# Agent attention with two feed-forward layers on one core: output transfers later in SyncE's order, one layer end in two pieces, a written order for the last nine half groups

## The chip, the cores and the metric

The kernel runs on one core of one Trainium2 chip. The metric is the device time of one execution in microseconds (us). Five engines work side by side, each in its own order: TensorE (PE; its weight loads are listed as PEld), VectorE (DVE), ScalarE (ACT), GpSimd (POOL) and SyncE (SP). SyncE computes nothing; here it issues transfers and passes on signals.

## The reference

For 12480 tokens of 128 values each, and 49 agent rows, all float32:

```python
a2k = softmax(scale * agents @ k.T)          # 49 x 12480
agent_v = a2k @ v                            # 49 x 128
x = softmax(scale * q @ agents.T) @ agent_v  # 12480 x 128
h = x @ w_in                                 # first layer, 128 -> 2048
x = (h / (1 + exp(-h))) @ w_out              # 2048 -> 128
h = x @ w2_in                                # second layer, 128 -> 2048
out = (h * cos(h)) @ w2_out                  # 2048 -> 128
```

The weights are float64 in memory and are split into a high and a low float32 part; so are the activations. A product of a split pair is three matmuls: high by high, low by high, high by low.

## The kernel before

The first 110 us or so load and transpose k, q and v, split the weights and do the attention. All that follows, and all that the change touches, is the two layers.

The tokens stand in 25 tiles t (22 of 512, then 416, 416 and 384). The 2048 inner values stand in 16 chunks of 128; a half group (g, k), with g = 4t + m, is two of these chunks of one tile. So a tile has eight half groups, and there are 200 in all. For each half group the first layer does `L1_h` (PE), `L1_act` (ACT, silu), `L1_hi` (ACT, high part), `L1_lo` (DVE, low part) and `L1_y` (PE, adds into the bank y1 of the tile). The second layer does, with x2 as its input, `L2_h` (PE), `L2_n` (ACT, line 789: whole turns of the cosine's argument), `L2_r` (DVE, 799: what is left of it), `L2_cos` (ACT, 808), `L2_g` (DVE, 816: times h), `L2_hi` (825, high part: DVE, but ACT for k = 1 of the last groups), `L2_lo` (POOL, 834) and `L2_y` (PE, into the bank y2).

The main loop (line 883) runs over steps s. A step does the first layer of half group s and the second layer of half group u = s - 11; a round is eight steps, one tile. Once a round the first layer of a tile ends: ACT copies the high part of bank y1 (`x2h`, 751), DVE subtracts it (`x2l`, 759). The bank y1 may be written again only when both have read it. And once a round a tile of the second layer ends (`L2_end`): DVE transposes bank y2 into tile `o` (856), and SyncE issues four transfers of `o` to the output (858). Also once a round SyncE issues two transfers that load `x3` (614).

In the main loop every product runs on half of TensorE's rows (`half`, line 621): the upper 64 rows do one stream of products, the lower 64 the same stream nine products later, side by side. [...]

```python
n = nc.sync.nop()
tc.add_manual_dep(n.ins, other[1], AFTER, reason="one row tile at a time in a bank")
tc.add_manual_dep(i.ins, n.ins.name, AFTER, reason="one row tile at a time in a bank")
```

It waits for the last product of the one half in that bank, and the first product of the other half waits for it. I call it a fence. There are about five in a step, and SyncE takes fences and transfers strictly in the order written. The kernel up to the end of the main loop stands in that written order on every engine (`tc.manual_schedule()`, opened at 220 and closed by `whole.close()` at 909).

After the main loop come nine half groups of the second layer alone (u = 191 to 199, the loop at 915), on whole rows (`whole_rows`, 734). There a scheduler sets the order on each engine.

Of the kernel before, what the change touches and what calls it, by code (L numbers as in the profile page):

```python
# [8 lines left out]
F32 = mybir.dt.float32  # L9
# [5 lines left out]
ALU = mybir.AluOpType  # L15
# [14 lines left out]
WIDE = 512  # L30
# [39 lines left out]
def agent_attention_moe_moe_kernel(ctx, tc, q, k, v, agents, w_in, w_out, w2_in, w2_out, out):  # L70
    nc = tc.nc
# [44 lines left out]
    def b32(ap):  # L116
        return ap.bitcast(F32)
# [23 lines left out]
    whole = ctx.enter_context(ExitStack())  # L141

    edge = ctx.enter_context(tc.tile_pool(name="edge", bufs=1, side="right"))
    edge.tile([128, EDGE // 4], F32, name="border")
    x3_p = ctx.enter_context(tc.tile_pool(name="x3", bufs=2, side="right"))
    late = ctx.enter_context(ExitStack())

    def after(name, bufs):
# [408 lines left out]
    with ExitStack() as ml:  # L557
# [11 lines left out]
        NL = len(widths)  # L569
        NG = NL * 4  # L570

        def toks(t):
            return widths[t]
# [10 lines left out]
        h1s, g1s, y1s, x2s, h2s, c2s, g2s, y2s = {}, {}, {}, {}, {}, {}, {}, {}  # L584
        v, sc, gp = nc.vector, nc.scalar, nc.gpsimd
# [5 lines left out]
        def wide(pool, tag, dt, g):  # L591
            return pool.tile([128, 2, WIDE], dt, tag=tag, name=tag)[:, :, :toks(g // 4)]

        last_pair, taken = [], [0]
# [26 lines left out]
        def half(x, bank, n, out, w, g, start, stop):  # L621

            assert before[0] is None or before[0][0] == x or before[0][1] != bank
            before[0] = x, bank
            rows = slice(HALF * x, HALF * x + n)
            i = nc.tensor.matmul(  # L626
                out=out, lhsT=w[rows], rhs=g[rows], start=start, stop=stop, tile_position=(HALF * x, 0)
            )
            other = writer.get((bank, 1 - x))
            if other is not None and other[0] > fenced[0]:  # L630
# [3 lines that stand above are left out]
                fenced[0] = other[0]  # L634
            writer[bank, x] = count[0], i.ins.name
            count[0] += 1
# [8 lines left out]
        def level():  # L645
            while behind:
                half(1, *behind.pop(0))
# [97 lines left out]
        def L1_end_a(g):  # L745

            if not (0 <= g < NG and g % 4 == 3):
                return
            t = g // 4
            xh = x2_p.tile([128, WIDE], F32R, tag="x2h", name="x2h")[:, :toks(t)]  # L750
            sc.copy(out=xh, in_=y1s[t])
            x2s[t] = [xh]

        def L1_end_b(g):
            if not (0 <= g < NG and g % 4 == 3):
                return
            t = g // 4
            xl = x2_p.tile([128, WIDE], F32R, tag="x2l", name="x2l")[:, :toks(t)]
            v.tensor_tensor(out=xl, in0=y1s.pop(t), in1=b32(x2s[t][0]), op=ALU.subtract)  # L759
            x2s[t].append(xl)  # L760


        def L2_h(g, k, how=whole_rows, bank=pair_bank):
            if not 0 <= g < NG:
                return
            t, m = g // 4, g % 4
            h = bank()
            xh, xl = x2s[t]
            ops = []
            for j in range(2):  # L770
                c = 4 * m + 2 * k + j
                y = h[:, j, :toks(t)]
                ops += [
                    (("h2", g, k, j), y, i2h[:, c, :], xh, True, False), (("h2", g, k, j), y, i2l[:, c, :], xh, False, False),
                    (("h2", g, k, j), y, i2h[:, c, :], xl, False, True),
                ]
            how(ops)
            h2s[g, k] = h[:, :, :toks(t)]
# [5 lines left out]
        def L2_n(g, k):  # L784
            if not 0 <= g < NG:
                return
            n = wide(n_p, "n", I32, g)
            for p in parts(g):
                sc.activation(  # L789
                    out=n[:, p], in_=h2s[g, k][:, p], func=AF.Identity, scale=1.0 / (2.0 * PI), bias=quarter  # L790
                )
            c2s[g, k] = n

        def L2_r(g, k):
            if not 0 <= g < NG:
                return
            n = c2s[g, k]
            for p in parts(g):
                v.scalar_tensor_tensor(  # L799
                    out=b32(n)[:, p], in0=n[:, p], scalar=-2.0 * PI, in1=h2s[g, k][:, p], op0=ALU.mult, op1=ALU.add  # L800
                )

        def L2_cos(g, k):
            if not 0 <= g < NG:
                return
            r = b32(c2s[g, k])
            for p in parts(g):
                sc.activation(out=r[:, p], in_=r[:, p], func=AF.Sin, bias=halfpi)  # L808

        def L2_g(g, k):  # L810
            if not 0 <= g < NG:
                return
            r, h = b32(c2s.pop((g, k))), h2s.pop((g, k))
            f = wide(g2_p, "g2", F32, g)
            for p in parts(g):
                v.tensor_tensor(out=f[:, p], in0=r[:, p], in1=h[:, p], op=ALU.mult)  # L816
            g2s[g, k] = [f]

        def L2_hi(g, k):

            if not 0 <= g < NG:
                return
            gh = wide(g2h_p, "g2h", F32R, g)
            for p in parts(g):
                (sc.copy if k and g + LAG >= NG else v.tensor_copy)(out=gh[:, p], in_=g2s[g, k][0][:, p])  # L825
            g2s[g, k].append(gh)

        def L2_lo(g, k):
            if not 0 <= g < NG:
                return  # L830
            f, gh = g2s[g, k]
            gl = wide(g2l_p, "g2l", F32R, g)
            for p in parts(g):
                i = (v if (g, k) == (NG - 1, 1) else gp).tensor_tensor(  # L834
                    out=gl[:, p], in0=f[:, p], in1=b32(gh)[:, p], op=ALU.subtract
                )
            if last_lo[0] is not None:
                tc.add_manual_dep(i.ins, last_lo.pop().ins.name, AFTER, reason="one at a time on the port to SBUF")
                last_lo.append(None)
            g2s[g, k] = [gh, gl]  # L840
# [10 lines left out]
        def L2_end(g):  # L851
            if not (0 <= g < NG and g % 4 == 3):
                return
            t = g // 4
            o = o_p.tile([128, WIDE // 32, 32], F32, tag="o", name="o")[:, :toks(t) // 32]
            v.transpose(out=o.rearrange("p b j -> p (b j)"), in_=y2s.pop(t))  # L856
            for cb in range(4):
                (nc.scalar if t == 24 and cb % 2 else nc.sync).dma_start(  # L858
                    out=out[span(t), 32 * cb:32 * cb + 32].rearrange("(b i) j -> i b j", i=32),
                    in_=o[32 * cb:32 * cb + 32],  # L860
                )

        def first_products(g):
            if g == 1:
# [12 lines left out]
        o_p = pool("o", 2, "right")  # L877
        LEAD = 2 * LAG + 1

        def at(s):  # L880
            return s // 2, s % 2

        for s in range(2 * LAG, 2 * NG + 2):
            u = s - LEAD
            steady[0] = int(u >= 3)
            if s % 8 == 2:
                swapped_in(s // 8 + 1)
            L2_h(*at(u), both_halves, bank2)
            if s % 8 == 6:
                L2_end(at(u - 4)[0])  # L890
            L2_hi(*at(u - 2))
            if s > 2 * LAG:
                L1_lo(*at(s - 2))
            L2_lo(*at(u - 2))
            L1_h(*at(s))
            if s > LEAD and s % 8 == 2:
                L1_end_a(at(s - 3)[0])
            L1_hi(*at(s - 1))
            if s > LEAD and s % 8 == 2:
                L1_end_b(at(s - 3)[0])  # L900
            L2_g(*at(u - 1))
            L2_y(*at(u - 3), both_halves)
            L1_y(*at(s - 2), both_halves)
            L2_n(*at(u))
            L2_r(*at(u))
            L1_act(*at(s))
            L2_cos(*at(u))
        level()
        whole.close()
        L1_end_a(NG - 1)  # L910
        L1_end_b(NG - 1)
        taken[0] = 2
        L2_hi(*at(2 * NG - LEAD))
        L2_lo(*at(2 * NG - LEAD))
        for s in range(2 * NG + 2, 2 * NG + LEAD + 4):
            u = s - LEAD
            L2_g(*at(u - 1))
            L2_y(*at(u - 3))
            L2_h(*at(u))
            L2_hi(*at(u - 1))  # L920
            L2_n(*at(u))
            L2_r(*at(u))
            L2_lo(*at(u - 1))
            if s % 8 == 5:
                L2_end(at(u - 3)[0])
            L2_cos(*at(u))


# [28 lines left out]
```

## Time and profile before

| | |
|---|---|
| time, three runs | 1130.25, 1131.27 (median), 1132.8 us |
| profiled execution | 1131.86 us, span of its instructions 1130.1 us |
| PE busy | 1077.7 us, 95% of the span |
| DVE busy | 919.9 us, 81% |
| ACT busy | 903.6 us, 80% |
| POOL busy | 503.2 us, 45% |
| mean granted clock of TensorE | 0.995 |

The span runs from the first to the last instruction; the rest of the execution's time lies around it. Busy is the time in which an engine worked on something; matmul ends are modelled. [...]

### The profile page before, as it was taken

Reading aid. Unit: us, or ns where it says so; the run is one execution under the profiler, and the core shown is the slowest. Engines: PE = TensorE matmul, PEld = TensorE weight load, DVE = VectorE, ACT = ScalarE, POOL = GpSimd, SP = SyncE. Lnnn points to the kernel's source line nnn. Section 1 sums busy time; section 2 is a strip of 40 time slices with the busy share of each in tenths; the row PEclk is TensorE's granted clock in tenths of the full one; section 3 lists DMA queues with packets and bytes.
Section 4 is the critical chain, followed back from the end, with each engine's and each line's share of the span. In section 5 each row is a group of like instructions: output and inputs, shape, how many; then the busy total and the mean of one; then the engine's idle time right before and its main releaser. Section 6 shows DMA issues by size and latency. Waiting matters only on the chain.

```text
span 1130.1 us, 22554 instructions
## 1 busy us (share of the span) xinstructions
PE 1077.7 (95%) x9069; PEld 931.7 (82%) x9069; DVE 919.9 (81%) x1050; ACT 903.6 (80%) x968; POOL 503.2 (45%) x251
## 2 busy tenths in 40 slices
PE   9999999999999999999999999999999999999996
PEld 5897698788888888798888888888888888888985
DVE  6877787888887888888888787888788888878876
ACT  5888887887887787788788788778878878777865
POOL 0443054444444454445454444454445444445444
PEclk9999999999999999999999999999999999999999
DMA  9872000000000000000000000000000000000000
GB/s 350 306 246 94 8 8 10 18 9 10 18 9 10 17 9 18 11 9 17 10 9 18 11 13 13 10 18 8 14 14 8 18 10 8 16 10 16 2 8 15
DMA packets 67058, 40.32 MB, mean 36 GB/s; under 512 B 52774, under 2 KB 57501, under 8 KB 66953
## 3 DMA queue, kind: packets, MB, share of 16 engines
q1 hardware_dynamic: 66152, 38.78, 11.5%
q8 instruction: 71, 1.16, 0.4%
q14 instruction: 35, 0.28, 0.1%
q10 hardware_dynamic: 800, 0.10, 0.1%
HBM read 27.58 MB, written 6.39 MB: 30 GB/s over the span
## 4 chain that ended last, share of the span: by engine, by line
PE 75%; DVE 10%; ACT 6%; SPq 4%; issue 3%; DMA 1%; POOL 0%; DVEq 0%; POOLq 0%; ACTq 0%
PE h L626 39%; PE y L626 27%; ACT n L789 5%; SPq L858 4%; DVE n L799 3%; DVE g1l L718 2%; PE h L252 2%; PE h L364 2%; DVE o L856 1%; PE y L734 1%; DVE g2h L825 1%; DVE x2l L759 1%; PE h L288 1%; PE y L351 1%; PE y L422 1%
## 5 line engine op out<-in xcount | busy, mean ns | idle before, releaser
L834 POOL TENSOR_TENSOR g2l<-g,g2h 128x1024 fp32r<-128x1024 f32 (+2 forms) x200 | 468.5, 2343 | 552.1 <-DVE g1l L718 534.9
L799 DVE SCALAR_TENSOR_TENSOR n<-n,h 128x1024 f32<-128x1024 int32 (+3 forms) x202 | 238.9, 1184 | 173.5 <-ACT n L789 170.4
L626 PE MATMUL h<-x2h,i2h 64*128 64x512 f32 (+1 forms) x764 | 296.7, 388 | 35.7 <-SPq L631 34.8
L789 ACT ACTIVATE n<-h,quarter 128x1024 int32<-128x1024 f32 (+3 forms) x202 | 219.5, 1088 | 112.8 <-PE h L626 82.8
L626 PE MATMUL y<-g1h,o1h 64*128 64x512 f32 (+2 forms) x768 | 297.9, 388 | 1.4 <-DVE x2l L759 0.4
L626 PE MATMUL y<-g1h,o1l 64*128 64x512 f32 (+2 forms) x768 | 296.3, 386 | 0.0
L626 PE MATMUL y<-g2h,o2l 64*128 64x512 f32 (+1 forms) x752 | 296.0, 394 | 0.0
L626 PE MATMUL y<-g2h,o2h 64*128 64x512 f32 (+1 forms) x752 | 294.3, 391 | 0.0
L626 PE MATMUL h<-x2h,i2l 64*128 64x512 f32 (+1 forms) x764 | 293.7, 384 | 0.0
L626 PE MATMUL h<-x2l,i2h 64*128 64x512 f32 (+1 forms) x764 | 293.4, 384 | 0.0
L808 ACT ACTIVATE n<-n,halfpi 128x1024 f32<-128x1024 f32 (+3 forms) x202 | 226.9, 1124 | 79.7 <-DVE n L799 79.6
L718 DVE TENSOR_TENSOR g1l<-g,g1h 128x1024 fp32r<-128x1024 f32 (+2 forms) x200 | 238.2, 1191 | 4.3 <-ACT g1h L710 1.6
L816 DVE TENSOR_TENSOR g<-n,h 128x1024 f32<-128x1024 f32 (+3 forms) x202 | 237.4, 1176 | 4.4 <-ACT n L808 3.7
L626 PE MATMUL y<-g2l,o2h 64*128 64x512 f32 (+1 forms) x752 | 233.4, 390 | 0.0
L626 PE MATMUL y<-g1l,o1h 64*128 64x512 f32 (+2 forms) x768 | 232.9, 383 | 0.2 <-DVE g1l L718 0.2
L710 ACT CAST g1h<-g 128x1024 fp32r<-128x1024 f32 (+2 forms) x200 | 203.0, 1015 | 0.2
L703 ACT ACTIVATE g<-h 128x1024 f32<-128x1024 f32 (+2 forms) x200 | 199.6, 998 | 2.4 <-DVE g1l L718 1.2
L626 PEld LDWEIGHTS h<-x2h,i2h 64*128 64x128 f32 x764 | 141.0, 185 | 55.9 <-SPq L631 43.2
L626 PE MATMUL h<-pT,w2h 49*128 49x512 f32 (+2 forms) x400 | 158.2, 397 | 0.0
L626 PEld LDWEIGHTS y<-g1h,o1h 64*128 64x128 f32 x768 | 142.4, 185 | 16.8 <-DVE x2l L759 11.4
L626 PE MATMUL h<-x,w2h 49*128 49x512 f32 (+2 forms) x400 | 155.7, 391 | 0.0
L626 PEld LDWEIGHTS h<-x2l,i2h 64*128 64x128 f32 x764 | 140.9, 184 | 13.0
(145 smaller groups left out, 1921.4 us busy)
## 6 DMA issues: line engine op xcount, KB each, us to landing
qraw<-in_q_dram SPq DMA_DIRECT2D x12, 512.0 KB
vraw<-in_v_dram SPq DMA_DIRECT2D x12, 512.0 KB
kraw<-in_k_dram SPq DMA_DIRECT2D x11, 512.0 KB
out_dram<-o SPq DMA_DIRECT2D x88, 64.0 KB
x<-pT SPq DMA_DIRECT2D x44, 98.0 KB
wraw<-in_moe_w_in_dram SPq DMA_DIRECT2D x8, 512.0 KB
wraw<-in_moe_w_out_dram SPq DMA_DIRECT2D x8, 512.0 KB
kraw<-in_k_dram SPq DMA_DIRECT2D x2, 256.0 KB
```

Source lines behind the costliest of these rows:

```text
L252: nc.tensor.transpose(out=pt[:, g, p * s:p * s + p], in_=r[:, h * g + s, :], identity=ident[:p, :p])
L364: nc.tensor.matmul(out=ps[:p, NA * i:NA * i + 2 * NA], lhsT=xt[:, i // h, p * (i % h):p * (i % h) + p], rhs=ag2, start=True, stop=True,)
L626: i = nc.tensor.matmul(out=out, lhsT=w[rows], rhs=g[rows], start=start, stop=stop, tile_position=(HALF * x, 0))
L703: sc.activation(out=f, in_=h1s.pop((g, k))[:, :, :toks(g // 4)], func=AF.Silu)
L710: sc.copy(out=gh, in_=g1s[g, k][0])
L718: i = v.tensor_tensor(out=gl, in0=f, in1=b32(gh), op=ALU.subtract)
L789: sc.activation(out=n[:, p], in_=h2s[g, k][:, p], func=AF.Identity, scale=1.0 / (2.0 * PI), bias=quarter)
L799: v.scalar_tensor_tensor(out=b32(n)[:, p], in0=n[:, p], scalar=-2.0 * PI, in1=h2s[g, k][:, p], op0=ALU.mult, op1=ALU.add)
L808: sc.activation(out=r[:, p], in_=r[:, p], func=AF.Sin, bias=halfpi)
L816: v.tensor_tensor(out=f[:, p], in0=r[:, p], in1=h[:, p], op=ALU.mult)
L834: i = (v if (g, k) == (NG - 1, 1) else gp).tensor_tensor(out=gl[:, p], in0=f[:, p], in1=b32(gh)[:, p], op=ALU.subtract)
L858: (nc.scalar if t == 24 and cb % 2 else nc.sync).dma_start(out=out[span(t), 32 * cb:32 * cb + 32].rearrange("(b i) j -> i b j", i=32), in_ ...
```

## The change

The diff has these parts. `L2_end` keeps the transpose; the four transfers move into a new `L2_out`, which the main loop calls at the end of the same step, so that on SyncE they stand behind four more fences. The copy and the subtraction at the end of the first layer become two instructions each, one for each half of the tile's columns (`cuts`). The last nine half groups are now inside the written order (`whole.close()` stands at the very end), and that order is a new one: in each step `L2_y` of u - 3, then `L2_h` of u, then `L2_n` of u, `L2_cos` of u - 1, `L2_g`, `L2_hi` and `L2_lo` of u - 2. The pool of `x3` gets another rule for the reuse of its buffers. ACT's two output transfers of the last tile are the same.

```diff
--- before.py
+++ after.py
@@ -142,7 +142,7 @@
 
     edge = ctx.enter_context(tc.tile_pool(name="edge", bufs=1, side="right"))
     edge.tile([128, EDGE // 4], F32, name="border")
-    x3_p = ctx.enter_context(tc.tile_pool(name="x3", bufs=2, side="right"))
+    x3_p = ctx.enter_context(tc.tile_pool(name="x3", bufs=2, side="right", reuse_waits="tile"))
     late = ctx.enter_context(ExitStack())
 
     def after(name, bufs):
@@ -748,7 +748,8 @@
                 return
             t = g // 4
             xh = x2_p.tile([128, WIDE], F32R, tag="x2h", name="x2h")[:, :toks(t)]
-            sc.copy(out=xh, in_=y1s[t])
+            for c in cuts(t):
+                sc.copy(out=xh[:, c], in_=y1s[t][:, c])
             x2s[t] = [xh]
 
         def L1_end_b(g):
@@ -756,9 +757,14 @@
                 return
             t = g // 4
             xl = x2_p.tile([128, WIDE], F32R, tag="x2l", name="x2l")[:, :toks(t)]
-            v.tensor_tensor(out=xl, in0=y1s.pop(t), in1=b32(x2s[t][0]), op=ALU.subtract)
+            y = y1s.pop(t)
+            for c in cuts(t):
+                v.tensor_tensor(out=xl[:, c], in0=y[:, c], in1=b32(x2s[t][0])[:, c], op=ALU.subtract)
             x2s[t].append(xl)
 
+        def cuts(t):
+            h = toks(t) // 2
+            return slice(0, h), slice(h, toks(t))
 
         def L2_h(g, k, how=whole_rows, bank=pair_bank):
             if not 0 <= g < NG:
@@ -852,13 +858,21 @@
             if not (0 <= g < NG and g % 4 == 3):
                 return
             t = g // 4
-            o = o_p.tile([128, WIDE // 32, 32], F32, tag="o", name="o")[:, :toks(t) // 32]
-            v.transpose(out=o.rearrange("p b j -> p (b j)"), in_=y2s.pop(t))
+            outs[t] = o_p.tile([128, WIDE // 32, 32], F32, tag="o", name="o")[:, :toks(t) // 32]
+            v.transpose(out=outs[t].rearrange("p b j -> p (b j)"), in_=y2s.pop(t))
+
+        def L2_out(g):
+            if not (0 <= g < NG and g % 4 == 3):
+                return
+            t = g // 4
+            o = outs.pop(t)
             for cb in range(4):
-                (nc.scalar if t == 24 and cb % 2 else nc.sync).dma_start(
+                (nc.scalar if t == NL - 1 and cb % 2 else nc.sync).dma_start(
                     out=out[span(t), 32 * cb:32 * cb + 32].rearrange("(b i) j -> i b j", i=32),
                     in_=o[32 * cb:32 * cb + 32],
                 )
+
+        outs = {}
 
         def first_products(g):
             if g == 1:
@@ -905,25 +919,33 @@
             L2_r(*at(u))
             L1_act(*at(s))
             L2_cos(*at(u))
+            if s % 8 == 6:
+                L2_out(at(u - 4)[0])
         level()
-        whole.close()
+        taken[0] = 2
+        TAIL = 2 * NG + 2 - LEAD
+        u = TAIL - 1
         L1_end_a(NG - 1)
+        L2_g(*at(u))
         L1_end_b(NG - 1)
-        taken[0] = 2
-        L2_hi(*at(2 * NG - LEAD))
-        L2_lo(*at(2 * NG - LEAD))
-        for s in range(2 * NG + 2, 2 * NG + LEAD + 4):
-            u = s - LEAD
-            L2_g(*at(u - 1))
+        L2_hi(*at(u - 1))
+        L2_lo(*at(u - 1))
+        for u in range(TAIL, 2 * NG + 3):
             L2_y(*at(u - 3))
             L2_h(*at(u))
-            L2_hi(*at(u - 1))
             L2_n(*at(u))
+            if u > TAIL:
+                L2_cos(*at(u - 1))
+            if u > TAIL + 1:
+                L2_g(*at(u - 2))
+            if u % 8 == 2:
+                L2_end(at(u - 3)[0])
+                L2_out(at(u - 3)[0])
+            if u > TAIL:
+                L2_hi(*at(u - 2))
+                L2_lo(*at(u - 2))
             L2_r(*at(u))
-            L2_lo(*at(u - 1))
-            if s % 8 == 5:
-                L2_end(at(u - 3)[0])
-            L2_cos(*at(u))
+        whole.close()
 
 
 # ---- launch: one core; inputs and outputs as the reference has them ----
```

How this moves instructions at the end of the first layer, on DVE, in the middle of the main loop. `x2l` is the low part, `x2h` the high part that ACT copies; in brackets what an instruction waits for. Before:

```order
L718 TENSOR_TENSOR g1l_8008<-g1_7921,g1h_7951 128x1024
L759 TENSOR_TENSOR x2l_8023<-y1_7505,x2h_8019 128x512 [waits Activation_49]
L816 TENSOR_TENSOR g2_8025<-n_7983,h2_7924 128x1024 [waits Pool_49]
L799 SCALAR_TENSOR_TENSOR n_8057<-n_8057,h2_7992 128x1024 [waits Activation_49]
L825 CAST g2h_8077<-g2_8025 128x1024 [waits DVE_49]
```

And in the changed kernel (another tile, the same place in the round):

```order
L718 TENSOR_TENSOR g1l_7494<-g1_7407,g1h_7437 128x1024
L762 TENSOR_TENSOR x2l_7510<-y1_6991,x2h_7505 128x256 [waits PE_49,Activation_49]
L762 TENSOR_TENSOR x2l_7510<-y1_6991,x2h_7505 128x256
L822 TENSOR_TENSOR g2_7513<-n_7469,h2_7410 128x1024 [waits Pool_49]
L805 SCALAR_TENSOR_TENSOR n_7545<-n_7545,h2_7478 128x1024 [waits Activation_49]
```

One subtraction of 512 columns has become two of 256; the first waits for ACT, the second has no wait of its own.

On PE in the last nine half groups, from the middle of `L2_h` of u = 193. `h2_14469`, `h_14492` and `h2_14509`, `h_14532` are u = 193 and 194 in the one and the other kernel, `y2_...` is the output bank, `g2h` and `g2l` the high and low part. Before:

```order
L734 MATMUL h2_14469<-x2h_14407,i2l_75 128x384
L734 MATMUL h2_14469<-x2l_14409,i2h_74 128x384
L734 MATMUL h_14492<-x2h_14407,i2h_74 128x384
L734 MATMUL h_14492<-x2h_14407,i2l_75 128x384
L734 MATMUL h_14492<-x2l_14409,i2h_74 128x384
L734 MATMUL h_14492<-x2h_14407,i2h_74 128x384
L734 MATMUL h_14492<-x2h_14407,i2l_75 128x384
L734 MATMUL y2_14188<-g2h_14453,o2h_76 128x416
```

And now:

```order
L734 MATMUL h2_14509<-x2h_14454,i2l_75 128x384
L734 MATMUL h2_14509<-x2l_14459,i2h_74 128x384
L734 MATMUL y2_14232<-g2h_14521,o2h_76 128x416
L734 MATMUL y2_14232<-g2h_14521,o2l_77 128x416
L734 MATMUL y2_14232<-g2h_14521,o2h_76 128x416
L734 MATMUL y2_14232<-g2h_14521,o2l_77 128x416
L734 MATMUL y2_14232<-g2l_14523,o2h_76 128x416 x2
L734 MATMUL h_14532<-x2h_14454,i2h_74 128x384
```

All six products of `L2_y` of u = 191 now stand ahead of `L2_h` of u = 194; five of the six of that `L2_h` stood ahead of them before.

On ACT, a little later (`h_14492` to `h2_14545` are u = 194 to 196, `h2_14585` and `h_14608` are u = 196 and 197). Before:

```order
L789 ACTIVATE n_14501<-h_14492,quarter_67 128x2x384
L808 ACTIVATE n_14478<-n_14478,halfpi_68 128x2x384
L808 ACTIVATE n_14501<-n_14501,halfpi_68 128x2x384
L789 ACTIVATE n_14531<-h2_14522,quarter_67 128x2x384
L825 CAST g2h_14499<-g2_14484 128x2x384
L808 ACTIVATE n_14531<-n_14531,halfpi_68 128x2x384
L789 ACTIVATE n_14554<-h2_14545,quarter_67 128x2x384
```

And now:

```order
L795 ACTIVATE n_14592<-h2_14585,quarter_67 128x2x384
L814 ACTIVATE n_14569<-n_14569,halfpi_68 128x2x384
L795 ACTIVATE n_14615<-h_14608,quarter_67 128x2x384
L814 ACTIVATE n_14592<-n_14592,halfpi_68 128x2x384
L831 CAST g2h_14620<-g2_14618 128x2x384
```

The high part of u - 2 now always follows `L2_n` of u and the cosine of u - 1. The fences themselves are only waits and stand in no such list.

## Rows read from the trace of the kernel before

**Rows 1.** Waits of the whole run: who waited for whom; us in total, times, longest.

```profile
PEld h L626 <- SPq L631: 44.6, 28, 2.4
...
PEld y L626 <- DVE x2l L759: 11.4, 24, 0.6
```

**Rows 2.** Timeline, one output (start us, us, engine, line, operation, idle before).

```profile
593.19 0.71 DVE L856 STREAM_TRANSPOSE o<-y 128x512 f32<-128x512 f32 x1
...
593.93 1.95 SPq L858 DMA_DIRECT2D out_dram<-o  x4
...
595.99 0.18 PEld L626 LDWEIGHTS h<-x2h,i2h 64*128 64x128 f32 x1 [1.85 <-SPq L631]
```

**Rows 3.** Timeline, around one load of x3.

```profile
570.59 0.39 PE L626 MATMUL y<-g2l,o2h 64*128 64x512 f32 x1
...
571.14 1.50 SPq L614 DMA_DIRECT2D x<-pT  x2
...
572.88 0.19 PEld L626 LDWEIGHTS y<-g1h,o1h 64*128 64x128 f32 x1
...
573.11 0.39 PE L626 MATMUL y<-g1h,o1h 64*128 64x512 f32 x1
```

**Rows 4.** Timeline, marks of the rounds and of the steps.

```profile
348.66 0.18 PEld L626 LDWEIGHTS h<-x2h,i2h 64*128 64x128 f32 x1 [2.44 <-SPq L631]
...
391.19 0.18 PEld L626 LDWEIGHTS h<-x2h,i2h 64*128 64x128 f32 x1 [1.84 <-SPq L631]
...
561.53 1.12 ACT L789 ACTIVATE n<-h,quarter 128x1024 int32<-128x1024 f32 x1 [0.32 <-PE h L626]
...
571.20 1.12 ACT L789 ACTIVATE n<-h,quarter 128x1024 int32<-128x1024 f32 x1 [0.33 <-PE h L626]
...
576.04 0.18 PEld L626 LDWEIGHTS y<-g1h,o1h 64*128 64x128 f32 x1 [0.47 <-DVE x2l L759]
```

**Rows 5.** Stretches: us, busy of PE, PEld, DVE, ACT, POOL; PEclk; DMA share; GB/s.

```profile
350.10:353.60 3.50, 3.50 (x21) 3.05 (x20) 2.09 (x3) 2.97 (x3) 0.15 (x1) 0.51 0.00 0
1005.50:1008.90 3.40, 3.40 (x20) 3.16 (x19) 0.70 (x1) 1.84 (x2) 1.21 (x1) 0.51 0.02 5
1104.90:1107.20 2.30, 0.12 (x1) 0.00 (x0) 2.30 (x4) 2.09 (x3) 0.80 (x1) 1.00 0.00 0
1107.90:1111.30 3.40, 3.40 (x13) 3.40 (x12) 2.46 (x4) 1.28 (x2) 2.72 (x3) 0.51 0.40 67
```

**Rows 6.** Groups by shape: busy us, mean ns of one | idle before.

```profile
L759 DVE TENSOR_TENSOR x2l<-y,x2h 128x512 fp32r<-128x512 f32 x22 | 15.2, 691 | 0.3 <-ACT x2h L751 0.2
...
L834 POOL TENSOR_TENSOR g2l<-g,g2h 128x768 fp32r<-128x768 f32 x6 | 11.0, 1838 | 7.7 <-DVE g2h L825 6.2 <-ACT g2h L825 1.4
...
L808 ACT ACTIVATE n<-n,halfpi 128x768 f32<-128x768 f32 x6 | 5.6, 931 | 2.3 <-DVE n L799 2.3
...
L789 ACT ACTIVATE n<-h,quarter 128x768 int32<-128x768 f32 x6 | 5.4, 897 | 3.1 <-PE h L734 3.1
...
L825 ACT CAST g2h<-g 128x768 fp32r<-128x768 f32 x3 | 2.5, 828 | 0.2 <-DVE g L816 0.2
...
L759 DVE TENSOR_TENSOR x2l<-y,x2h 128x384 fp32r<-128x384 f32 x1 | 0.6, 550 | 0.0
```

**Rows 7.** Timeline, the last nine half groups.

```profile
1092.07 0.52 PE L626 MATMUL y<-g1l,o1h 64*128 64x384 f32 x2
...
1113.11 0.34 PE L734 MATMUL h<-x2h,i2h 128*128 128x384 f32 x1
1113.29 0.34 PE L734 MATMUL h<-x2h,i2l 128*128 128x384 f32 x1
...
1120.90 1.06 ACT L789 ACTIVATE n<-h,quarter 128x384 int32<-128x384 f32 x2 [0.36 <-PE h L734]
...
1121.98 1.97 POOL L834 TENSOR_TENSOR g2l<-g,g2h 128x384 fp32r<-128x384 f32 x2 [0.39 <-DVE g2h L825]
...
1125.37 0.58 PE L734 MATMUL y<-g2l,o2h 128*128 128x384 f32 x2
```

## The prediction

> **What bounds the kernel now.** I read the page first: TensorE is busy for 95% of the span, so time can come only from its few waits and from its clock. Then the waits of the whole run [rows 1]. Two groups return every round. PE's weight loads wait for SyncE 28 times, 44.6 us in all, and for the subtraction `x2l` 24 times, 11.4 us. In time order 23 of the waits for SyncE stand one per round and are like the one of 1.85 us in rows 2 (2.44 and 1.84 in rows 4); the other five are short and early.
>
> The timeline of one round shows why [rows 2]. The transpose of an output tile ends at 593.90. SyncE, which has stood at the first transfer until then, issues the four transfers from 593.93 to 595.88. The next fence is behind them, and PE's next weight load starts at 595.99, 0.11 us after the last issue, having been idle for 1.85 us. What is held up is a fence, not data.
>
> A round lasts (595.99 - 391.19) / 5 = 40.96 us [rows 2, 4], from one mark to another five rounds on. A step without a wait lasts (571.20 - 561.53) / 2 = 4.835 us, so eight last 38.68. Of the 2.28 us beyond that, 0.47 are the wait for `x2l` at 576.04 [rows 4], and 1.81 are the transfers.
>
> The clock is the third loss. [...]
>
> **The change part by part.** Sums are made against the profiled execution's 1131.86 us; the median of the runs is 0.59 lower.
>
> *Transfers.* They move behind four fences, to the fence that waits for the last upper product of `L2_y`; the next fence is that of `L1_y`. The trace has these two fences with transfers between them already: the x3 load stands there. Its row shows the budget [rows 3]. The upper product that releases the first fence starts at 570.59 and ends at 570.98; SyncE issues from 571.14 to 572.64; the weight load that needs the second fence starts at 572.88 with no wait. With four output transfers, 1.95 us instead of 1.50, SyncE would be done at 573.09, and the load 0.11 later at 573.20 instead of 572.88. The load is 0.32 late. Its matmul starts 0.23 after it now, at 573.11, and a load takes 0.19 [rows 3]: PE loses between 0.09 us, if a matmul may start with its load, and 0.28, if the load must end first. I take the middle, 0.19. The data do not hold SyncE any more: the product that releases the first fence writes bank y2 anew, so the transpose that reads this bank is over. Bounds: 0, if a load may lag further, and 0.45 (1.95 - 1.50), if the x3 load only just fits. So 1.81 - 0.19 = 1.62 us per round, 23 rounds: -37.3 us (bounds -41.6 and -31.3). Queued behind the transfers on SyncE are only fences and, four steps on, the x3 load; its `reuse_waits` I cost at nothing, since no one waits for it [rows 3] and its data are for the next round. The output buffer has a spare and is written again two rounds later.
>
> *Clock in the main loop.* With waits of 0.2 instead of 1.9 to 2.4 us I expect no stretch at half clock there: two stretches of 1.57, and the 0.59 by which the wait of 348.66 was longer than the others [rows 4]: -3.7 us (bounds -3.7 and 0).
>
> *Two pieces at the end of the first layer.* PE waits there for the end of `x2l` [rows 4]. The gain could come only if the first subtraction began when the first copy is done. The order rows deny it: the second subtraction has no wait for ACT, so the first waits for both copies. What is left is the cost of more instructions. DVE: 691 ns at 512 columns and 550 at 384 [rows 6] make 1.10 ns per column and 128 ns fixed; two pieces cost 128 more, less the overlap of neighbours (estimated at 0.08), about 0.05 us. The same on ACT's copy, 0.04. So +0.09 x 24 = +2.2 us. Upper bound: a pair of 384 columns on ACT takes 1.06 [rows 7] where 768 take 0.897 [rows 6], 0.16 more; with 0.06 on DVE that is 0.22 x 24 = +5.3. Lower bound: the whole wait of 11.4 goes.
>
> [...]
>
> *The last nine half groups.* Before, they run from the end of the main loop's last product (1092.07 + 0.52 = 1092.6) [rows 7] to the end of the span at 1130.1: 37.5 us. In the new order PE may not begin `L2_h` of u before `L2_y` of u - 3 is done, and that waits for POOL's low part. POOL waits for ACT's high part, and ACT does that one only after `L2_n` of u and the cosine of u - 1. This closes a loop over two half groups, since ACT has the high part of every second one: n 0.90, cosine 0.93, high part 0.83, low part on POOL 1.84 [rows 6], then on PE the last two products of `L2_y`, six of `L2_h`, six of `L2_y`, six of `L2_h`, twenty at 0.18 (1113.11 to 1113.29 [rows 7]): 3.6. Sum 8.1; the four hand-overs of about 0.1 each and the overlaps of neighbours on ACT and in the rounding roughly cancel (estimate). The chain begins with twelve products (2.3 us) and goes four times around from u = 191 to 199: 32.4 (the first rounds are of 416 columns, which I count the same). After the last `L2_h`: two pieces of n 1.06 and of the cosine about as much, high part 0.83, POOL's low parts of two half groups 1.84 and 1.97, seven products 1.2, and from the last product on what it is now, 1130.1 - 1125.95 = 4.15: 12.2 with the hand-overs [rows 6, 7]. Sum 46.9, so +9.4 us at full clock.
>
> PE then stands idle between its groups for n, cosine and high part, 2.7 us in each of four loops, a little longer than the idle that went before the stretch at 1107.9 [rows 5]. Each stretch at half clock costs up to half of its 3.4 us. Between none and four, I take 4 us beyond the one that is in the 37.5 already. So +13.4 (bounds 0, since PE waits in the order before too, as from 1104.9 to 1107.2 [rows 5], and +23.4, below).
>
> **Sum.** -37.3 - 3.7 + 2.2 + 13.4 = -25.4: 1131.86 - 25.4 = 1106.5, and 0.6 lower against the median: **1106 us**.
>
> **The rivals.**
>
> *The tail runs at half clock throughout.* Then the twenty products of each loop cost 3.6 us more, some 14 over four loops instead of my 4: 1116 us. For it: the idle of 2.7 us per loop. Against it: that stretch ended at 1111.3, with half of the last half groups still to come [rows 5, 7]. [...]
>
> *The tail is no longer than before*, because other waits were in it that go: 1106 - 13.4 = 1093 us. For it: PE waits now too. Against it: the loop closes by the order rows themselves.
>
> *The two pieces do what they say*: copy and subtraction overlap and the wait of 0.47 goes. 1106 - 2.2 - 11.4 = 1092 us at the most. Against it: the order rows.
>
> *The wait is moved, not shortened*: the four issues take long enough to hold the next fence as well. Price: the first term vanishes, as may the second; with the tail and the pieces 1131.3 + 2.2 + 13.4 = 1147 us, slower. It decides from where a round still loses 1.3 us (23 x 0.52 + 3.7 = 15.6), that is, where the four issues take 3.0 us. For it: one issue after the other is in SyncE's way again. Against it: 1.95 us in the row, and the x3 load that nobody waits for [rows 2, 3].
>
> **How the numbers follow.** The forecast 0.62, the tail at half clock 0.15, the tail no longer 0.10, the pieces 0.05, the wait moved 0.08. The range 1096 to 1118 takes in the bounds of the transfers (1102 to 1112) and the half clock, and about half of the gain of the two better cases. Runs of this kernel differ by 0.2%, 2.3 us; all cases but the last are faster by far more: faster 0.91, same 0.01, slower 0.08.
>
> **What would show it.** Right: waits for SyncE in the main loop of 0.1 to 0.5 us; rounds of about 39.4 us; `x2l` waits of 0.5 to 0.6 us; no stretch at half clock before the tail; from the last half-row product to the end 46 to 53 us, with PE waiting for POOL's `g2l` and ACT's `g2h` ahead of every second `L2_y`. Wrong: rounds above 40.4 us (the wait has moved), `x2l` waits below 0.4 (the pieces overlap), a tail below 40 us (the loop does not close).

## The result, and the profile after

The changed kernel takes 1115.33 us (median of 4 runs, 1114.46 to 1116.01) beside 1130.76 us before: a ratio of 0.986 [0.984, 0.988], 15.4 us less. The forecast was 1106 us, in a range of 1096 to 1118. The sign was right; the gain is three fifths of the one forecast.

The profiled execution (1114.46 us, span 1112.7) divides at the end of the main loop's last product. Before, that was at 1092.6, and 37.5 us followed [rows 7]. Now it is at 1059.06 + 0.52 = 1059.6, and 53.1 follow. So the main loop gained 33.0 us (38.8 forecast) and the last nine half groups lost 15.6 (13.4 forecast).

These are the waits of PE in the whole run after the change (total us, times, longest), the answer to [rows 1]:

```profile
PEld y L626 <- PE h L626: 15.2, 23, 0.8
...
PEld y L734 <- ACT g2h L831: 11.9, 4, 3.2
PEld y L626 <- SPq L631: 11.3, 26, 1.1
...
PEld y L734 <- POOL g2l L840: 7.3, 8, 1.5
...
PE y L626 <- DVE x2l L762: 6.4, 23, 0.4
```

The 44.6 us for SyncE (L631, the fences) have become 11.3, and they now stand ahead of a product of `L1_y`. The 11.4 for `x2l` have become 15.2: the first row, put down to PE's own `h`, is the wait for bank y1, since the matmul behind each of these loads is listed as waiting for `x2l` (the last row). New are four waits for ACT's `g2h`, of about 3 us each.

The timeline of two rounds shows the place of the transfers and the end of a tile:

```profile
560.54 0.18 PEld L626 LDWEIGHTS y<-g1h,o1h 64*128 64x128 f32 x1 [0.66 <-PE h L626]
...
580.32 2.77 SPq L870 DMA_DIRECT2D out_dram<-o  x4
...
583.20 0.18 PEld L626 LDWEIGHTS y<-g1h,o1h 64*128 64x128 f32 x1 [1.14 <-SPq L631]
...
599.42 0.65 ACT L752 CAST x2h<-y 128x256 fp32r<-128x256 f32 x2
600.10 0.76 DVE L762 TENSOR_TENSOR x2l<-y,x2h 128x256 fp32r<-128x256 f32 x2
600.97 0.18 PEld L626 LDWEIGHTS y<-g1h,o1h 64*128 64x128 f32 x1 [0.66 <-PE h L626]
...
620.76 1.94 SPq L870 DMA_DIRECT2D out_dram<-o  x4
...
622.81 0.18 PEld L626 LDWEIGHTS y<-g1h,o1h 64*128 64x128 f32 x1 [0.32 <-SPq L631]
640.57 0.18 PEld L626 LDWEIGHTS y<-g1h,o1h 64*128 64x128 f32 x1 [0.66 <-PE h L626]
```

At 620.76 SyncE issues for 1.94 us, and the load stands 0.11 us behind the last issue, after 0.32 us in which no load ran. At 580.32 the same four issues take 2.77 us, and that time is 1.14. The two copies take 0.65 us where one took 0.59, the two subtractions 0.76 instead of 0.69, and the first subtraction starts 0.03 us after the second copy. A round from mark to mark is 640.57 - 600.97 = 39.60 us; the one before it, with the long issues, is 600.97 - 560.54 = 40.43. Its load waited 0.82 us more than the other, and the round is 0.83 longer.

The last nine half groups, over one loop of two of them:

```profile
1059.06 0.52 PE L626 MATMUL y<-g1l,o1h 64*128 64x384 f32 x2
...
1079.62 0.90 ACT L795 ACTIVATE n<-h,quarter 128x768 int32<-128x768 f32 x1 [0.83 <-PE h L734]
...
1080.42 0.93 ACT L814 ACTIVATE n<-n,halfpi 128x768 f32<-128x768 f32 x1
...
1081.24 0.82 ACT L831 CAST g2h<-g 128x768 fp32r<-128x768 f32 x1
...
1082.14 1.82 POOL L840 TENSOR_TENSOR g2l<-g,g2h 128x768 fp32r<-128x768 f32 x1 [4.28 <-ACT g2h L831]
...
1089.36 0.90 ACT L795 ACTIVATE n<-h,quarter 128x768 int32<-128x768 f32 x1 [0.77 <-PE h L734]
```

It is the loop of the prediction, n, cosine, high part, low part, products, and lasts 9.74 us instead of 8.1. Two stretches of it (PE, PEld, DVE, ACT, POOL busy; the granted clock of TensorE as a share of full speed; DMA):

```profile
1079.60:1082.10 2.50, 0.00 (x0) 0.00 (x0) 1.79 (x3) 2.44 (x3) 0.00 (x0) 1.00 0.00 0
...
1084.60:1087.60 3.00, 3.00 (x11) 3.00 (x11) 0.00 (x0) 0.73 (x1) 1.78 (x1) 0.50 0.00 0
```

PE is idle while ACT works (granted clock 1.00), and afterwards about half of its products run at a granted clock of 0.50. Such a stretch of 3 to 4 us came in three loops, and one of 6.8 us (1101.3 to 1108.1) near the end. In the main loop there was none, as three windows over it show. One stretch of 3.4 us at half clock would make such a window 0.99, as it does in the kernel before from 120 to 433. (The profile's own row of the granted clock, in tenths and slices of 28 us, is too coarse for this: in the kernel before it reads 9 even where [rows 5] have 0.51.)

```profile
120.00:433.00 313.00, 309.75 (x2602) 278.03 (x2602) 265.78 (x276) 264.66 (x271) 143.72 (x60) 1.00 0.06 12
433.00:746.00 313.00, 310.19 (x2650) 285.27 (x2649) 268.65 (x277) 264.55 (x269) 152.25 (x64) 1.00 0.06 13
746.00:1059.00 313.00, 309.36 (x2768) 286.79 (x2765) 268.69 (x289) 261.25 (x278) 153.37 (x67) 1.00 0.06 12
```

### The profile page after: what moved, and what is told of

Its sections match the earlier page's. It is cut to its first block, busy times and chain, and to the rows that moved or that the text cites. A ratio compares the mean times of both kernels' runs of the same rounds, so it can differ in the third digit from the quotient of the medians.

```text
span 1112.7 us, 22648 instructions
## 1 busy us (share of the span) xinstructions
PE 1078.6 (97%) x9069; PEld 967.7 (87%) x9069; DVE 927.0 (83%) x1075; ACT 906.5 (81%) x993; POOL 503.1 (45%) x251
## 4 chain that ended last, share of the span: by engine, by line
PE 83%; ACT 8%; DVE 5%; SPq 2%; issue 1%; POOL 1%; DMA 1%; POOLq 0%; ACTq 0%; DVEq 0%
PE y L626 41%; PE h L626 31%; ACT n L795 3%; ACT n L814 3%; DVE n L805 3%; PE h L252 2%; PE y L734 2%; PE h L364 2%; DVE x2l L762 2%; SPq L870 1%; ACT x2h L752 1%; PE h L288 1%; PE y L351 1%; POOL g2l L840 1%; PE y L422 1%
## 5 line engine op out<-in xcount | busy, mean ns | idle before, releaser
L626 PEld LDWEIGHTS y<-g1h,o1h 64*128 64x128 f32 x768 | 141.9, 185 | 32.9 <-PE h L626 15.2
L626 PEld LDWEIGHTS h<-x2h,i2h 64*128 64x128 f32 x764 | 140.6, 184 | 11.3 <-DVE g L822 2.5
L626 PEld LDWEIGHTS y<-g1l,o1h 64*128 64x128 f32 x768 | 141.2, 184 | 7.3 <-DVE g1l L718 0.6
```

Of the source, the lines that this page charges most:

```text
L626: i = nc.tensor.matmul(out=out, lhsT=w[rows], rhs=g[rows], start=start, stop=stop, tile_position=(HALF * x, 0))
```

## The experiments

Times are medians; a ratio is against the kernel before in runs on the same chip, one such set for experiments 1 to 4, one for 5 to 8 and one for 9 and 10. Of each edit the lines that matter are shown; `...` stands for others.

**1. The transfers alone.**

```diff
...
             L2_cos(*at(u))
+            if s % 8 == 6:
+                L2_out(at(u - 4)[0])
...
```

> The kernel before with the late output transfers alone: one copy and one subtraction, the last nine half groups ordered by the scheduler. Theory: the main loop gives 1.81 - 0.38 = 1.43 us per round, 23 rounds, and 3.7 us of clock, so 36.6 us: 1094 us, with one wait for SyncE of 0.3 to 0.35 us per round and the wait for x2l back at 0.47. By the size in the prediction (0.19 left per round) it is 1090. Rival: the residual wait for SyncE in the changed kernel comes from its two pieces or from the reuse rule of x3; then it is gone here and the time is 1085.

1095.64 us, ratio 0.969 [0.968, 0.971]: 35.2 us less. The wait for SyncE is there without the pieces and without the rule for x3, and `x2l` is back at 0.47:

```profile
519.74 0.18 PEld L626 LDWEIGHTS y<-g1h,o1h 64*128 64x128 f32 x1 [0.47 <-DVE x2l L759]
...
541.58 0.18 PEld L626 LDWEIGHTS y<-g1h,o1h 64*128 64x128 f32 x1 [0.34 <-SPq L631]
559.13 0.18 PEld L626 LDWEIGHTS y<-g1h,o1h 64*128 64x128 f32 x1 [0.47 <-DVE x2l L759]
```

The rival falls. This part alone beats the changed kernel by 20 us.

**2. The two pieces alone.**

```diff
+            for c in cuts(t):
+                sc.copy(out=xh[:, c], in_=y1s[t][:, c])
...
```

(and the subtraction likewise.)

> The kernel before with the copy and the subtraction in two pieces alone. Theory: the first subtraction waits for both copies, and the wait for x2l grows from 0.47 to 0.66 us, 24 times: 1130.8 + 4.6 = 1135 us. By the prediction's size (+0.09 per round) 1133. Rival: the pieces overlap, the wait shrinks, and the time is below 1128.

1137.62 us, ratio 1.006 [1.005, 1.008]: 6.8 us more. The rival falls: the pieces do not overlap. The wait is 0.65 to 0.66 us in most rounds and the round 41.16 us (598.82 - 557.66) instead of 40.96:

```profile
557.66 0.18 PEld L626 LDWEIGHTS h<-x2h,i2h 64*128 64x128 f32 x1 [1.84 <-SPq L631]
...
578.86 0.18 PEld L626 LDWEIGHTS y<-g1h,o1h 64*128 64x128 f32 x1 [0.65 <-PE h L626]
598.82 0.18 PEld L626 LDWEIGHTS h<-x2h,i2h 64*128 64x128 f32 x1 [1.85 <-SPq L631]
```

24 times 0.19 are 4.6 us, just below the interval (5.5 to 8.9 us). The two profiled executions (1137.42 and 1131.86 us) differ by 5.6 us, of which 5.3 lie in the main loop: its last product ends at 1097.33 + 0.52 = 1097.85 here and at 1092.6 before. The rest of the 6.8 is not settled; it is no more than the runs of the kernel before differ among themselves (1128.2 to 1131.29).

**3. The written order of the last nine half groups alone.**

```diff
-        whole.close()
...
+        for u in range(TAIL, 2 * NG + 3):
             L2_y(*at(u - 3))
             L2_h(*at(u))
             L2_n(*at(u))
+            if u > TAIL:
+                L2_cos(*at(u - 1))
...
+        whole.close()
```

> The kernel before with the written order of the last nine half groups alone. Theory: these last 53 us instead of 37.5: 1146 us, with four waits of PE of about 2.9 us for ACT's g2h. Rival: in the changed kernel the longer end is an effect of the other two parts (the pieces of the last tile, transfers); then it is about 38 us here and the time is 1131.

1145.36 us, ratio 1.014 [1.012, 1.016]: 14.5 us more. From the last half-row product to the end of the span (1143.4) it is 53.3 us, with the same four waits for `g2h`, 11.9 us in all. The order makes the loss by itself.

```profile
1089.61 0.52 PE L626 MATMUL y<-g1l,o1h 64*128 64x384 f32 x2
```

The three parts alone add up to -13.9 us; the changed kernel has -15.4. The rule for x3's buffers was not run alone, but there is little room for an effect of it: 39.39 us for a round with the transfers alone and 0.19 for the pieces make 39.58, and the changed kernel has 39.60.

**4. The transfers two and two.**

```diff
...
+            if s % 8 in (6, 7):
+                L2_out(at(u - 4 - (s % 8 == 7))[0], (0, 1) if s % 8 == 6 else (2, 3))
...
```

> As the run with late transfers alone, but two of the four are issued at the end of step 6 of a round and two at the end of step 7, each pair between the same two fences of its step. Theory: two issues take about 1.0 us, less than the 1.5 us that fit between the two fences; no wait for SyncE is left and 0.38 us per round are won against the late transfers alone: 1094 - 8.7 = 1085 us. Rival: any transfer in that place costs PE the wait, by the hand-over itself and not by the length of the issues; then there are two such waits per round and the time is 1094 or more.

1083.26 us, ratio 0.959 [0.957, 0.960]: 12.4 us below the first experiment, more than the 8.7 expected. A pair of issues takes 0.85 us, and but for one wait of under 0.2 us no load waits for them in any round:

```profile
554.12 0.18 PEld L626 LDWEIGHTS y<-g1h,o1h 64*128 64x128 f32 x1 [0.47 <-DVE x2l L759]
...
593.18 0.18 PEld L626 LDWEIGHTS y<-g1h,o1h 64*128 64x128 f32 x1 [0.46 <-DVE x2l L759]
...
612.98 0.85 SPq L864 DMA_DIRECT2D out_dram<-o  x2
```

A round lasts 593.18 - 554.12 = 39.06 us, against 559.13 - 519.74 = 39.39 in experiment 1. So a listed wait of 0.34 us costs the round 0.33 us, all of it, as in the two rounds of the changed kernel above. Over 23 rounds that is 7.6 of the 12.4 us. Most of the rest are rounds in which the load of experiment 1 waited longer than 0.34, once 1.87 us behind four issues of 3.46 (at 894.96); these waits add up to some 3.9 us more.

**5. Extra matmuls in the idle stretches of the last nine half groups.** They are added work; nothing reads their result.

```diff
...
+        def filled(ops):
+            fill(14)
+            whole_rows(ops[:4])
+            fill(5 if u < 200 else 2)
+            whole_rows(ops[4:])
...
+            L2_y(*at(u - 3), filled if u in (194, 196, 198, 200) else whole_rows)
...
```

(`fill(n)` issues n matmuls.)

> The changed kernel with extra matmuls in the last nine half groups, whose results no one reads (into the free bank y1): 14 ahead of L2_y of u = 191, 193, 195, 197, where PE waits 2.9 us for ACT's g2h, and 5 (2 the last time) ahead of their two low products, where it waits 1.3 us for POOL's g2l. Theory: half of the clock costs 1.6 us or more in each of the four loops; with PE at work these stretches go, and the end takes 47 us instead of 53: 1109 us, granted clock 1.0 in the loops. Rival: the loop over n, cosine, high part and low part alone sets the time and the clock costs nothing; then the time stays at 1115, or is more, since the extra products stand ahead of real ones.

1112.60 us, ratio 0.984 [0.982, 0.986]. The clock behaved as expected; the time only in half. From 1059.9 to 1108.0 the granted clock is 1.00:

```profile
1059.90:1108.00 48.10, 40.06 (x200) 34.23 (x199) 29.55 (x36) 21.63 (x31) 18.94 (x11) 1.00 0.05 9
```

The end takes 1109.6 - 1060.0 = 49.6 us instead of 53.1: the clock cost 3.5 us, or a little more if the extra products held up real ones (the medians differ by 2.7, the intervals overlap). With full clock the end is still 2.7 us longer than the 46.9 worked out in the prediction: n follows n after 10.1, 8.6 and 8.6 us (from 1069.61, 1079.72 and 1088.28) where the prediction had 8.1. The loops show why:

```profile
1074.89 0.62 DVE L862 STREAM_TRANSPOSE o<-y 128x416 f32<-128x416 f32 x1 [2.50 <-PE y L734]
1075.44 0.52 DVE L831 CAST g2h<-g 128x768 fp32r<-128x768 f32 x1
1076.13 1.83 POOL L840 TENSOR_TENSOR g2l<-g,g2h 128x768 fp32r<-128x768 f32 x1 [1.97 <-DVE g2h L831]
...
1078.01 0.30 PEld L734 LDWEIGHTS y<-g2l,o2h 128*128 128x128 f32 x2 [1.35 <-POOL g2l L840]
...
1082.54 1.96 DVE L831 CAST g2h<-g 128x768 fp32r<-128x768 f32 x1
...
1084.67 1.84 POOL L840 TENSOR_TENSOR g2l<-g,g2h 128x768 fp32r<-128x768 f32 x1 [0.58 <-DVE g2h L831]
...
1086.56 0.30 PEld L734 LDWEIGHTS y<-g2l,o2h 128*128 128x128 f32 x2 [0.36 <-POOL g2l L840]
```

Once DVE's transpose waits 2.50 us for PE with the next high part queued behind it, and in the other loops DVE's high part takes 1.96 us instead of 0.52, beside POOL's low part. Either way POOL is late a second time in the loop and PE waits again.

**6. The high part first.** One edit in the changed kernel's order:

```diff
...
+            if u > TAIL + 1:
+                L2_g(*at(u - 2))
+            if u > TAIL:
+                L2_hi(*at(u - 2))
+                L2_lo(*at(u - 2))
             L2_n(*at(u))
...
```

(the same lines are taken out further down.)

> The changed kernel with one edit in the order of the last nine half groups: L2_g, L2_hi and L2_lo of u - 2 stand ahead of L2_n of u and L2_cos of u - 1, so that ACT makes the high part before these two. Theory: the length of the end comes from the order on ACT, high part behind n and cosine; with it ahead, the loop over two half groups becomes shorter by about 1.3 us (7 instead of 8.1, the same clock loss or a smaller one): the end 47 to 49 us, 1109 to 1111 us. Rival: the end is bound by PE's order (L2_y of u - 3 ahead of L2_h of u) whatever ACT does: 1115 us.

1108.80 us, ratio 0.981 [0.979, 0.983]: 6.5 us below the changed kernel's median. n follows n after 1084.00 - 1076.62 = 7.38 and 1091.37 - 1084.00 = 7.37 us:

```profile
1076.62 0.90 ACT L795 ACTIVATE n<-h,quarter 128x768 int32<-128x768 f32 x1 [3.83 <-PE h L734]
...
1084.00 0.90 ACT L795 ACTIVATE n<-h,quarter 128x768 int32<-128x768 f32 x1 [2.10 <-PE h L734]
...
1091.37 1.05 ACT L795 ACTIVATE n<-h,quarter 128x384 int32<-128x384 f32 x2 [2.10 <-PE h L734]
```

The end takes 1107.4 - (1059.79 + 0.52) = 47.1 us. These loops run at a granted clock of 1.00, so they are to be held against the 8.6 us of experiment 5: 1.2 us a loop come from the order on ACT, as expected. Much of the rest goes with the clock, which was low once in the loops (1073.2 to 1076.7) and not three times; the two were not parted further. So ACT's order sets the loop; PE's order, unchanged here, does not by itself. The edit also moves DVE's transpose at the end of a tile behind the high part; that falls outside the two loops shown.

**7. A third order of the last nine half groups, on experiment 4.**

```diff
...
+            for x in "i3 h0 r1 e5 n0 c1 g2 l3 y4".split():
...
```

(a letter for the step and the number of half groups that it lies behind: i, h, r, n, c, g, l, y are `L2_hi`, `L2_h`, `L2_r`, `L2_n`, `L2_cos`, `L2_g`, `L2_lo`, `L2_y`, and e is `L2_end` with its transfers.)

> The late transfers two and two (1083.3 us, its end of 37.9 us by the scheduler), with the last nine half groups in a third order, written by hand: in each step L2_hi of u - 3, L2_h of u, L2_r of u - 1, L2_n of u, L2_cos of u - 1, L2_g of u - 2, L2_lo of u - 3, L2_y of u - 4. The same instructions on the same engines. Theory: a written order is not slow as such; with L2_y one step later and the high part first the loop opens, the end takes 33 to 34 us and the time is 1079. Rival: written orders lose here because a wait on one engine holds what is queued behind it; then the end is 45 us or more and the time above 1090.

1079.74 us, ratio 0.956 [0.954, 0.957], the fastest of all runs here. The end takes 1079.7 - (1044.90 + 0.52) = 34.3 us, against 37.4 in experiment 4, where the scheduler made it. A written order is not slow as such. Of the four waits for `g2h` one of 0.3 us is left.

```profile
1044.90 0.52 PE L626 MATMUL y<-g1l,o1h 64*128 64x384 f32 x2
```

**8. ACT copies bank y1 whole; DVE works from the copy.**

```diff
...
+            sc.copy(out=xc, in_=y1s.pop(t))
...
+            v.tensor_copy(out=x2s[t][0], in_=x2s[t][1])
+            v.tensor_tensor(out=xl, in0=x2s[t][1], in1=b32(x2s[t][0]), op=ALU.subtract)
...
```

> The late transfers two and two (1083.3 us), and at the end of the first layer ACT copies bank y1 whole into SBUF; DVE makes x2h and x2l from that copy. It adds one DVE instruction per round, some 0.36 us. Theory: PE's wait for x2l (0.47 us, 24 times) is for the bank; the bank is free after ACT's copy, 0.7 us earlier, and the wait goes: 0.3 to 0.47 us per round, 1072 to 1076 us. Rival: the longer chain, or DVE's 0.36 us, is late for the next products of the second layer; then a wait for x2h, x2l or g takes the place and the time is 1083 or more.

1149.20 us, ratio 1.018 [1.015, 1.020]: 66 us more than experiment 4. The wait for the bank is gone; the rival was right that one for g takes its place, but it named neither the size nor the cause:

```profile
497.27 2.47 POOL L837 TENSOR_TENSOR g2l<-g,g2h 128x1024 fp32r<-128x1024 f32 x1 [2.43 <-DVE g1l L719]
497.52 2.76 DVE L762 TENSOR_TENSOR x2l<-x2c,x2h 128x512 fp32r<-128x512 f32 x1
...
500.21 1.21 DVE L819 TENSOR_TENSOR g<-n,h 128x1024 f32<-128x1024 f32 x1
...
501.47 0.18 PEld L627 LDWEIGHTS h<-x2h,i2h 64*128 64x128 f32 x1 [2.75 <-DVE g L819]
```

The subtraction takes 2.76 us instead of 0.69 and ends after POOL's instruction. Behind it on DVE is g, and PE waits 2.75 us for that. The next such load is at 542.86, so a round lasts 41.39 us, 2.33 more than in experiment 4: some 53 of the 66 us. The rest is the clock: eight stretches of 3 to 4 us at half clock stand in the main loop behind such waits (from 585.8 to 588.8 the granted clock is 0.50), where experiment 4 has none.

**9. The same, with POOL's low part of that step behind the subtraction.**

```diff
...
-            L2_lo(*at(u - 2))
+            if s % 8 != 2:
+                L2_lo(*at(u - 2))
...
+            if s % 8 == 2:
+                L2_lo(*at(u - 2))
...
```

(a signal also makes it wait for the subtraction.)

> The run with ACT's copy of bank y1 (1149.2 us) once more, with POOL's low part of that step (L2_lo) behind the subtraction x2l, so that the two do not run side by side. Theory: the subtraction took 2.76 us instead of 0.69 because both of its operands lay in SBUF and POOL worked on SBUF at the same time; alone it takes about 0.7 us, PE's wait of 2.75 us for g, queued behind it on DVE, goes, and with the bank free early the round falls from 39.08 to about 38.9 us: 1076 to 1081 us. Rival: the subtraction is slow by its operands, not by POOL; then it takes 2.7 us here too and the time stays near 1149.

1089.64 us, ratio 0.964 [0.963, 0.966]. The cause named for experiment 8 holds, the gain does not:

```profile
516.55 0.43 DVE L761 CAST x2h<-x2c 128x512 fp32r<-128x512 f32 x1
...
517.02 0.69 DVE L762 TENSOR_TENSOR x2l<-x2c,x2h 128x512 fp32r<-128x512 f32 x1
...
517.88 2.40 POOL L839 TENSOR_TENSOR g2l<-g,g2h 128x1024 fp32r<-128x1024 f32 x1 [3.55 <-DVE x2l L762]
...
518.89 0.18 PEld L627 LDWEIGHTS h<-x2h,i2h 64*128 64x128 f32 x1 [0.69 <-DVE g L821]
```

Alone the subtraction takes 0.69 us. The wait of 0.47 for the bank has turned into one of 0.69 for g, which has 0.43 us more of DVE's work ahead of it; the round is 39.3 us (from 518.89 to 558.23) against 39.06 in experiment 4.

**10. Experiments 9 and 7 together.** The edit is both of theirs.

> The run before with the third order of the last nine half groups as well (which gave 3.5 us): 1073 to 1078 us if its theory holds; near 1145 if the subtraction stays slow.

1086.60 us, ratio 0.962 [0.960, 0.964]: missed for the same reason as 9; the third order gave 3.0 us again.

## Why the prediction was right in sign and off in size

*Transfers.* The mechanism was right, and so was the place: the load that needs the next fence stands 0.11 us behind the last issue. The step that was mis-sized is "PE loses between 0.09 us, if a matmul may start with its load, and 0.28, if the load must end first. I take the middle, 0.19." PE loses 0.33 us (experiments 1 and 4). The rows of the changed kernel show how:

```profile
622.35 0.39 PE L626 MATMUL y<-g2l,o2h 64*128 64x512 f32 x1
...
622.81 0.49 PE L626 MATMUL y<-g1h,o1h 64*128 64x512 f32 x1
...
623.15 0.39 PE L626 MATMUL y<-g1h,o1l 64*128 64x512 f32 x1
```

The products of one stream follow one another every 0.23 us, each with its load about 0.23 ahead. So the load was due at 622.35 and its matmul at 622.58. Both start at 622.81, 0.46 and 0.23 late, and the next matmul follows after 0.34 instead of 0.23; 0.23 and 0.11 make the loss. That the listed wait is 0.32, as the prediction had it, is chance: it counts from the end of the last load, which is one of the other stream (622.31 + 0.18). The budget was too large because it was read in another step: from the start of the product that releases the fence to that of the matmul behind the next fence it is 2.52 us at the x3 load (570.59 to 573.11), and here it would be 2.37 (620.21 to 622.58). The delay of the load, 0.46, comes near the 0.45 of the prediction's bound, and PE loses 0.33 to 0.34 of it.

Besides, the 1.95 us for four issues was taken as fixed, and 6 of the 20 rounds of full width show waits of 0.44 to 1.14 us. Of the 11.3 us three early waits make 0.9; the rest is 0.45 per round. Transfers and clock alone gave 35.2 us (experiment 1) where 41.0 were forecast; that is the low bound of the transfers, 31.3, with the clock's 3.7.

*Clock in the main loop.* Right: no stretch at half clock was left there (granted clock 1.00 in all three windows). No run parts the term of 3.7 us from the transfers; what the trace of the kernel before shows of it is one round of 42.53 us (348.66 to 391.19 [rows 4]), 1.57 above the 40.96 of the others, with a stretch at a granted clock of 0.51 in it, and a second such stretch at 1005.5 [rows 5].

*Two pieces.* Right that they cost and why; the size was twice the forecast, 0.19 us per round instead of 0.09. Cutting cost 0.06 us on ACT and 0.07 on DVE, and the hand-over to the load grew from 0.06 to 0.11.

*The last nine half groups.* The loop closes as described; 53.1 us were measured and 50.9 forecast. The 4 us for the clock were about right (3.5, experiment 5), if they are taken for the whole loss: the text calls them 4 beyond the stretch that is in the 37.5 already, but adds them to a sum at full clock. The 46.9 at full clock were 2.7 too few: the sum followed ACT's high part only, and not DVE's, which is late behind the transpose or stretched beside POOL. That this makes the 2.7 is read from the rows of experiment 5; no run takes it away alone.

*The rivals.* Half clock throughout: no, a part of each loop, 3.5 us and not 14. The time alone would have spoken for it, since its 1116 us is the nearest to the measured 1115.33 of all the cases; that is chance, and only the trace and experiment 5 tell the two apart. Not every batch of products behind a wait began low: the one behind the wait of 2.97 us that ended at 1071.79 ran at a granted clock of 1.00 (1071.79 to 1073.00), and the next, behind 1.35 us at 1073.83, at 0.50 (1074.5 to 1077.1). An end no longer than before: no (experiment 3). Overlapping pieces: no (experiment 2). A wait that only moved: no, a quarter of it was left (10.4 of some 43 us in the rounds).

Of the signs that were named as right, the clock and most of the waits for SyncE (17 of 23 up to 0.5 us) came as stated, and the round of 39.60 us nearly; the waits for `x2l` were 0.66 us and not 0.5 to 0.6, and the end, 53.1, stands at the edge of 46 to 53. The 0.91 for faster counts any gain beyond the scatter of 2.3 us; for a gain of 2% (1108 us) it would not follow from the sum, since the range reaches to 1118 and the rival of half clock stands at 1116.

The forecast was 9.3 us too low. Against the parts run alone, 5.8 of that lie in the transfers, 4.6 in the pieces and 1.1 in the end; their sum is 2.2 more than the miss, about the scatter of the kernel before, whose medians in the four comparisons lay between 1129.35 and 1131.15.

## What to carry to other kernels

Where an engine in strict order passes signals for others, measure the room between two signals and put in only what fits with some spare: four issues of 1.95 us in a place where 1.5 had fitted cost 12 us a run against two and two, which left no such wait. Run the parts of a change alone: here two of three lost time, 6.8 and 14.5 us, and the gain of the third hid it. When an order is written by hand, look for the loop through all engines before the order is fixed; here an earlier place for the high part on ACT was worth 6.5 us with the clock that it gave back, and an order with one step more of distance for the high part, the low part and `L2_y` was 3 us better than the scheduler's.

## What the runs showed of the hardware that was not expected

A DVE subtraction with both operands in SBUF took 2.76 us when POOL's work had begun 0.25 us before it, and 0.69 alone (experiments 8 and 9), as in the kernel before, where one operand lay in PSUM and POOL began 0.19 us after it. `g`, with one operand in PSUM, took 1.21 us there though POOL's work had begun 0.42 us before it, as long as at 500.21 in experiment 8, where POOL was done (497.27 + 2.47 = 499.74). From the timeline of the kernel before:

```profile
575.29 0.69 DVE L759 TENSOR_TENSOR x2l<-y,x2h 128x512 fp32r<-128x512 f32 x1
...
575.48 2.40 POOL L834 TENSOR_TENSOR g2l<-g,g2h 128x1024 fp32r<-128x1024 f32 x1 [2.43 <-DVE g1l L718]
...
575.90 1.21 DVE L816 TENSOR_TENSOR g<-n,h 128x1024 f32<-128x1024 f32 x1
```

A DVE cast from SBUF to SBUF took 1.96 us beside POOL's low part and 0.52 otherwise (experiment 5). The expectation of experiment 8 had not reckoned with that. The kernel before keeps one such pair apart by a signal: line 838 makes POOL's low part wait for DVE's `g1l`, the 2.43 us in the row above; what it would take without that signal no run shows.

Why four issues of the same size took 1.94 us in most rounds and up to 3.46 in some (experiment 1) stays open.
